# One change at the hand-over from attention to feed-forward, in a two-layer transformer kernel on one core

## The chip, the cores and the metric

The kernel runs on one core of a Trainium2 chip. The core has five engines with a queue each, and every queue is worked off in order: TensorE (PE in the profile; its weight loads are listed apart as PEld), VectorE (DVE), ScalarE (ACT), GpSimd (POOL) and SyncE (SP), which here only issues transfers (DMAs). Matrix products land in PSUM, a memory of eight banks of 128 rows by 512 fp32 numbers; all other tiles lie in SBUF. The metric is the device time of one call in microseconds (us), and lower is better.

## What is computed

```python
x = x + A(layernorm(x)); x = x + B(layernorm(x))
x = x + A(layernorm(x)); x = x + B(layernorm(x))
# A: q = x@wq in 16 heads of 28; one k = x@wk and one v = x@wv for all heads
#    softmax(q k^T / sqrt(28)) v, heads side by side, @ wo
# B: (silu(x@w_gate) * (x@w_up)) @ w_down
```

x has 2048 rows (tokens) of 448 numbers; the feed-forward B is 1792 wide. Everything is fp32. The two layers have the same weights.

## The kernel before

The tokens are worked in four chunks (0 to 3) of 512, each of four tiles of 128 rows. Most products are made from numbers split in a high and a low part (names that end in h and l): high times high, high times low, low times high. The norm's output is turned over, so that features lie on the partitions; features 384 to 447 are the fourth block of a chunk's tile `xh`. There the high parts fill rows 0 to 63 and the low parts rows 64 to 127, and in the feed-forward a second copy of the high parts in rows 64 to 127 of another tile, `xd`, serves the upper half of the array.

**Attention.** For each chunk and each of four groups of four heads the kernel runs eight cycles, 128 cycles per layer (`cycle`). A cycle takes two tiles of 128 keys (y = 0 and 1). `tile_scores` (L640) makes the scores of four heads at once in four row strips of PE: three heads go to a PSUM tile of three banks (a "three"), the fourth to a bank of its own (a "single"). DVE copies each single to SBUF (`pair`, L661); ACT takes the exponential of the three (L662) of y = 0, of the three of y = 1, and then of both singles together (L663), in place. `pv` (L695) follows one cycle later with the product of the exponentials and the values, into one bank: for each key tile the three first, and then its half of the pair. DVE adds the bank to the group's sum `o` (L703). When a group's last cycle is done, `post` normalises it: a small DMA spreads the row sums (`rs`, L717), DVE takes the reciprocal, a DMA writes it to DRAM (`rd`, L727), another brings it back broadcast over the rows (L728), POOL multiplies (L734), four DMAs move rows between groups (L748), and POOL splits the result (`onh`, `onl`, L135 and L136). The product with `wo` can then run.

**Hand-over.** When the last cycle's `pv` is issued, the last group of chunk 3 still has that whole chain ahead of it. Meanwhile PE does work of the feed-forward on chunk 0, whose norm was made long before: `unit(0, 0, 0)` and `unit(0, 0, 1)`, with full-height products (L312). Behind the second stand the down product of the first unit (`down`, in two steps: the first right there, the second held back in `left`), the `wo` product of chunk 3's groups 0 to 2, the second step, the `wo` product of group 3, and the addition to x (L611). Then `rest` begins: DVE takes the norm's statistics of chunk 3 (L217, L218), POOL the factor 1/sqrt(variance + eps) of its four tiles (L222 and the power, L223), DVE applies it (L230) and turns the tiles (L268), and a DMA sends them out to come back feature-wise. POOL makes chunk 2's parts out of a load issued earlier. `begin` makes chunk 1's parts. The copies `xd` of chunks 0 and 1 are made by two DMAs (L127) at the head of `rest`.

**Feed-forward.** 14 blocks (`fc`) of 128 hidden features, in 7 groups of two; for each group all four chunks, and for each chunk two units. A unit makes gate and up (L332: 64-row products, two at a time in the lower and upper half of the array), ACT the SiLU (L1024), DVE the product with up (L1025), ACT the high part (L1028), DVE the low part (L1031). `down` makes h times w_down into four banks, one for each token tile: two steps of twelve 64-row products, lower and upper half side by side on different banks; after the first step four tiny ACT copies (`between`, L339) read the banks, since the second step uses the same banks from the other half. `self.flip`, turned over at each call, says which banks begin in the lower half. After a group's second unit the four banks are added to x: tile 0 by DVE (L901), tile 2 by an ACT copy (L904) and POOL (L905), tile 1 by DVE, tile 3 again by ACT and POOL. `by_tile` (L888) is the same down product in full rows, twelve products of 128 rows, tile after tile; before the change it serves only the very last group of the program.

The order on each engine is the order in which the Python code issues; nothing re-orders it. A tile pool that takes over the space of a closed pool makes the first user of the new tile wait for the last users of the old one. The program also holds a second, exact version of the forward pass behind a branch that these inputs don't take.

Of the kernel before, what the change touches and what calls it, by code (L numbers as in the profile page):

```python
# [55 lines left out]
def forward(  # L56
# [69 lines left out]
    def dma(dst, src):  # L126
        nc.sync.dma_start(dst.bitcast(F32), src.bitcast(F32))  # L127
# [82 lines left out]

    def norm_steps(c, pool=pers, twice=True):

        got = {}
        cs = slice(4 * c, 4 * c + 4)

        def stat(t):
            nc.vector.bn_stats(stats[:, 4 * c + t, :], xres[:, 4 * c + t, :])  # L217
            nc.vector.bn_aggr(mv[:, 4 * c + t, :], stats[:, 4 * c + t, :])  # L218

        def scale():  # L220
            rstd = pers.tile([P, 4], F32, name="rstd", bufs=2)
            nc.gpsimd.tensor_scalar(rstd, mv[:, cs, 1], 1.0, EPS, ALU.mult, ALU.add)  # L222
            nc.gpsimd.tensor_tensor(rstd, rstd, halfn, ALU.pow)  # L223
            got["r"] = rstd

# [7 lines left out]

        fs = [lambda t=t: stat(t) for t in range(4)] + [scale]
        return fs + [lambda t=t: apply(t) for t in range(4)], got
# [107 lines left out]
    class Attention:  # L343
# [229 lines left out]
        def scores(self, ff, xb):  # L573
            next(switch)
            inner = ExitStack()
            with tc.tile_pool(name=f"ow{self.layer}", bufs=1, side="right", reuse_waits="tile") as ow:
# [73 lines left out]
                pairs = [wp.tile([P, 2, 512], F32, name=f"pair{y}") for y in range(2)]  # L650

                def singles(m):

                    return banks[6 + m % 2], banks[7 - m % 2]

                def cycle(m):

                    es, copies, pair = [], [], pairs[m % 2]
                    for y, one in enumerate(singles(m)):
                        pt, pt1 = tile_scores(2 * m + y, threes[y], one)  # L660
                        copies.append(nc.vector.tensor_copy(pt1, one))  # L661
                        es.append(nc.scalar.activation(pt, threes[y], AF.Exp, scale=SCALE))  # L662
                    es.append(nc.scalar.activation(pair, pair, AF.Exp, scale=SCALE))  # L663
                    exps[m] = [e.ins for e in es]
# [125 lines left out]
                aside[NT // 2 * 15 + 5] = lambda: ff.fetch(1)  # L790
                last = NT // 2 * len(GR)
                for m in range(last):
# [33 lines left out]
                ff.begin(xb)  # L826
                due.pop(min(due))()
                ff.unit(0, 0, 0)
                due.pop(min(due))()
# [16 lines left out]
    class FeedForward:  # L846
# [6 lines left out]
        def down(self, fs, fc, d, hh, hl):  # L853


            _, _, dh, dl = self.W[fc]
            if self.layer == 1 and d is self.dn.get(NC - 1) and fs is groups[-1]:
                return [lambda: self.by_tile(fs, fc, d, ((hh, dh), (hh, dl), (hl, dh))), lambda: None]
            self.flip = 1 - self.flip
# [197 lines left out]
        def begin(self, xb):  # L1057

            self.x1p = xb.enter_context(tc.tile_pool(name=f"x1{self.layer}", bufs=1, reuse_waits="tile"))
            self.X[1] = xtile(self.x1p)  # L1060
            halved(self.X[1], self.got.pop(1), range(4), nc.scalar.copy, nc.vector.tensor_tensor)

        def rest(self, xb):
            self.stage = xb.enter_context(tc.tile_pool(name=f"stage{self.layer}", bufs=2, reuse_waits="tile"))
            self.xbp = xb.enter_context(tc.tile_pool(name=f"xb{self.layer + 1}", bufs=2, reuse_waits="tile"))
            xd = xb.enter_context(tc.tile_pool(name=f"xd{self.layer}", bufs=1, reuse_waits="tile"))
            self.xd = [xd.tile([P, 512], F32R, name=f"xd{c}") for c in range(NC)]
            for c in range(2):
                dma(self.xd[c][64:128, :], self.X[c][0][0:64, 3, :])
                self.X[c] = (*self.X[c][:2], self.xd[c])  # L1070
            t3 = ExitStack()
            own = t3.enter_context(tc.tile_pool(name=f"t3{self.layer}", bufs=1, reuse_waits="tile"))
            tb = own.tile([P, D // 32, P], F32, name="tb3")
            fs3, got = norm_steps(3, own, twice=False)
            for f in fs3[:5]:
# [118 lines left out]
```

## Time and profile before

| | us |
|---|---|
| median of 3 runs (lowest to highest) | 1949.36 (1948.67 to 1949.93) |
| the profiled execution | 1949.26 |
| its span, first to last instruction | 1947.5 |
| hand-over of layer 0, from the last `pv` to the first steady unit | about 555 to 595 of the span |
| hand-over of layer 1 | about 1518 to 1558 |

Times in the profile count from the first instruction. A row of the timeline gives start, duration, engine, line, operation, output<-inputs with shape, and in brackets how long the engine had stood idle and whom it waited for. Matmul durations are modelled: they overlap, so PE's pace is read from the distance between starts.

### The profile page before, as it was taken

To read this page: it belongs to the slowest core of one execution; us is meant where nothing else is said; L and a number is where in the kernel's file an instruction comes from. 1 tells how busy PE (TensorE), PEld (TensorE's weight loads), DVE (VectorE), ACT (ScalarE), POOL (GpSimd) and SP (SyncE) were. 2 spreads that over 40 slices of the span, in tenths; PEclk is the share of its full clock that TensorE was granted. 3 is DMA by queue.
4 is the path that set the end of the run, shared out by engine and by line. 5 is a ranking of instruction groups with operands and counts; after the bars stand their busy time and mean duration, and the time that the engine had idled before them with its cause. 6 is when DMAs were issued, how large, how long until landed. Compare 5 with 4: busy or idle time off the path is not lost. (4 is left out here: it accounts for less than half of the span.)

```text
span 1947.5 us, 43868 instructions
## 1 busy us (share of the span) xinstructions
PE 1934.0 (99%) x18393; PEld 1311.6 (67%) x18393; DVE 980.8 (50%) x1675; ACT 1251.9 (64%) x1871; POOL 560.1 (29%) x596
## 2 busy tenths in 40 slices
PE   9999999999999999999999999999999999999998
PEld 7544545445468999999974445454454688888887
DVE  6665575665754222322666555757657432232223
ACT  4899898998953333333359998989989333333332
POOL 4213123122215333433341221122231352333420
PEclk9999999999999999999999999999999999999999
DMA  5111011021122011100251110110221220011102
GB/s 166 57 35 30 22 40 41 23 58 31 32 81 73 17 32 32 33 22 22 63 157 43 34 34 21 40 39 24 57 50 31 77 62 25 17 32 32 33 1 77
DMA packets 105475, 87.54 MB, mean 45 GB/s; under 512 B 25304, under 2 KB 85464, under 8 KB 105272
## 3 DMA queue, kind: packets, MB, share of 16 engines
q1 hardware_dynamic: 103576, 83.25, 15.5%
q8 instruction: 145, 2.38, 0.5%
q10 hardware_dynamic: 1696, 1.43, 0.2%
q14 instruction: 58, 0.48, 0.1%
HBM read 59.48 MB, written 23.33 MB: 43 GB/s over the span
## 5 line engine op out<-in xcount | busy, mean ns | idle before, releaser
L662 ACT ACTIVATE pt<-three 128x1536 f32<-128x1536 f32 x512 | 731.2, 1515 | 52.7 <-PE three L640 52.7
L695 PE MATMUL bank<-pt,vsb 128*32 128x512 f32 x3072 | 490.8, 598 | 0.0
L695 PE MATMUL bank<-pair,vsb 128*32 128x512 f32 x1024 | 487.4, 598 | 0.6 <-ACT pair L663 0.6
L640 PE MATMUL bank<-qstack,keys 32*128 32x512 f32 x1536 | 471.8, 425 | 0.0
L640 PE MATMUL three<-qstack,keys 32*128 32x512 f32 x4608 | 428.7, 408 | 0.5 <-ACT stage L546 0.3
L640 PEld LDWEIGHTS bank<-qstack,keys 32*128 32x128 f32 x1536 | 243.3, 183 | 248.1 <-issue 124.6
L661 DVE COPY pair<-bank 128x512 f32<-128x512 f32 x512 | 354.3, 692 | 95.1 <-PE bank L640 60.0
L332 PE MATMUL bank<-xh,wgh 64*128 64x512 f32 x1712 | 357.4, 389 | 0.0
L1025 DVE TENSOR_TENSOR sg<-bank,sg 128x512 f32<-128x512 f32 x112 | 77.4, 691 | 485.4 <-ACT sg L1024 474.7
L332 PE MATMUL bank<-xh,wgl 64*128 64x512 f32 x1391 | 310.7, 390 | 0.0
L332 PE MATMUL bank<-wdh,h 64*128 64x448 f32 x1760 | 303.3, 363 | 1.0 <-DVE h L1031 0.6
L663 ACT ACTIVATE pair<-pair 128x1024 f32<-128x1024 f32 x256 | 289.6, 1131 | 0.0
L640 PEld LDWEIGHTS three<-qstack,keys 32*128 32x128 f32 x4608 | 261.8, 183 | 14.2 <-DVE xres L611 1.5
L332 PE MATMUL bank<-xl,wgh 64*128 64x512 f32 x1284 | 268.5, 389 | 0.0
L695 PEld LDWEIGHTS bank<-pt,vsb 128*32 128x32 f32 x3072 | 101.7, 109 | 246.2 <-issue 153.2
L905 POOL TENSOR_TENSOR xres<-stage,xres 128x448 f32<-128x448 f32 x107 | 126.7, 1204 | 480.5 <-ACT stage L904 480.2
L703 DVE TENSOR_TENSOR o<-bank,o 128x512 f32<-128x512 f32 x224 | 155.0, 692 | 202.3 <-PE bank L695 202.3
L339 ACT COPY seen<-bank 128x1 f32<-128x1 f32 x654 | 74.9, 164 | 253.3 <-PE bank L332 252.7
L1024 ACT ACTIVATE sg<-bank 128x512 f32<-128x512 f32 x112 | 67.2, 600 | 215.9 <-PE bank L332 210.8
L332 PEld LDWEIGHTS bank<-xh,wgh 64*128 64x128 f32 x1712 | 182.0, 184 | 18.4 <-issue 1.0
L332 PEld LDWEIGHTS bank<-wdh,h 64*128 64x128 f32 x1760 | 183.2, 184 | 15.5 <-issue 1.7
L332 PE MATMUL bank<-wdl,h 64*128 64x448 f32 x880 | 174.7, 367 | 0.0
(149 smaller groups left out, 2105.8 us busy)
## 6 DMA issues: line engine op xcount, KB each, us to landing
o<-rd SPq DMA_DIRECT2D x32, 256.0 KB
qraw<-qd SPq DMA_DIRECT2D x128, 56.0 KB
xt<-tb SPq DMA_DIRECT2D x32, 224.0 KB
wdr<-in_B_w_down_dram SPq DMA_DIRECT2D x28, 224.0 KB
xn<-xt SPq DMA_DIRECT2D x8, 768.0 KB
wr<-in_B_w_gate_dram SPq DMA_DIRECT2D x28, 192.0 KB
wr<-in_B_w_up_dram SPq DMA_DIRECT2D x28, 192.0 KB
qd<-stage SPq DMA_DIRECT2D x20, 224.0 KB
```

Source lines behind the costliest of these rows:

```text
L332: nc.tensor.matmul(po, a, b, start=start, stop=stop, skip_group_check=True)
L339: nc.scalar.copy(seen[:, i : i + 1], po[:, 0:1])
L640: nc.tensor.matmul(three[:, j, :] if j < 3 else one, k[js, kp, ks], q[js, part, :], start=(z == 0), stop=(z == 2), tile_position=(32 * j, 0),)
L661: copies.append(nc.vector.tensor_copy(pt1, one))
L662: es.append(nc.scalar.activation(pt, threes[y], AF.Exp, scale=SCALE))
L663: es.append(nc.scalar.activation(pair, pair, AF.Exp, scale=SCALE))
L695: nc.tensor.matmul(to[32 * j : 32 * j + 32, :], vsb[:, n % NT, :], pts[n][j], start=(y == 0), stop=(y == 1), skip_group_check=True,)
L703: f = nc.vector.tensor_tensor(accs[i][:, 0, :], to, accs[i][:, 0, :], ALU.add)
L905: nc.gpsimd.tensor_tensor(r, s, r, ALU.add)
L1024: nc.scalar.activation(in_order(sg, True), natural(pg[0], True), AF.Silu)
L1025: nc.vector.tensor_tensor(in_order(sg, True), natural(pg[1], True), in_order(sg, True), ALU.mult)
```

## The change

Four edits at the hand-over, in both layers alike.

1. In the last cycle of a layer the exponential of the two singles is issued between those of the two threes, instead of behind both.
2. The factors of chunk 3's norm (`norm_steps(..., each=True)`) are made tile by tile, each right behind its tile's statistics: four times two POOL instructions on one column, instead of two on four columns.
3. The two DMAs that make `xd` of chunks 0 and 1 move up from the head of `rest`: chunk 0's into `begin`, chunk 1's behind the first step of the last group's `post` chain. The pool of the `xd` tiles is opened in `begin` with them, and so lies in other space.
4. The first down product of a layer (block 0, chunk 0) is made by `by_tile` in one step, and nothing of it is held back. `self.flip` isn't turned in that call, so from there on each down product of the layer starts with the other assignment of banks to halves.

```diff
-    def norm_steps(c, pool=pers, twice=True):
+    def norm_steps(c, pool=pers, twice=True, each=False):
...
-        def scale():
-            rstd = pers.tile([P, 4], F32, name="rstd", bufs=2)
-            nc.gpsimd.tensor_scalar(rstd, mv[:, cs, 1], 1.0, EPS, ALU.mult, ALU.add)
-            nc.gpsimd.tensor_tensor(rstd, rstd, halfn, ALU.pow)
-            got["r"] = rstd
+        def scale(t0=0, n=4):
+            if "r" not in got:
+                got["r"] = pers.tile([P, 4], F32, name="rstd", bufs=2)
+            r = got["r"][:, t0 : t0 + n]
+            nc.gpsimd.tensor_scalar(r, mv[:, 4 * c + t0 : 4 * c + t0 + n, 1], 1.0, EPS, ALU.mult, ALU.add)
+            nc.gpsimd.tensor_tensor(r, r, halfn[:, 0:n], ALU.pow)
...
-        fs = [lambda t=t: stat(t) for t in range(4)] + [scale]
+        if each:
+            fs = [lambda t=t: (stat(t), scale(t, 1)) for t in range(4)] + [lambda: None]
+        else:
+            fs = [lambda t=t: stat(t) for t in range(4)] + [scale]
...
                         copies.append(nc.vector.tensor_copy(pt1, one))
+                        if y and m == last - 1:
+                            nc.scalar.activation(pair, pair, AF.Exp, scale=SCALE)
                         es.append(nc.scalar.activation(pt, threes[y], AF.Exp, scale=SCALE))
-                    es.append(nc.scalar.activation(pair, pair, AF.Exp, scale=SCALE))
+                    if m < last - 1:
+                        es.append(nc.scalar.activation(pair, pair, AF.Exp, scale=SCALE))
...
                 ff.begin(xb)
                 due.pop(min(due))()
+                ff.above(1)
                 ff.unit(0, 0, 0)
...
             if self.layer == 1 and d is self.dn.get(NC - 1) and fs is groups[-1]:
                 return [lambda: self.by_tile(fs, fc, d, ((hh, dh), (hh, dl), (hl, dh))), lambda: None]
+            if fc == 0 and d is self.dn[0]:
+                return [lambda: self.by_tile(fs, fc, d, ((hh, dh), (hh, dl), (hl, dh))), lambda: None]
             self.flip = 1 - self.flip
...
         def begin(self, xb):
 
             self.x1p = xb.enter_context(tc.tile_pool(name=f"x1{self.layer}", bufs=1, reuse_waits="tile"))
+            xd = xb.enter_context(tc.tile_pool(name=f"xd{self.layer}", bufs=1, reuse_waits="tile"))
+            self.xd = [xd.tile([P, 512], F32R, name=f"xd{c}") for c in range(NC)]
+            self.above(0)
             self.X[1] = xtile(self.x1p)
             halved(self.X[1], self.got.pop(1), range(4), nc.scalar.copy, nc.vector.tensor_tensor)
+
+        def above(self, c):
+
+            dma(self.xd[c][64:128, :], self.X[c][0][0:64, 3, :])
 
         def rest(self, xb):
...
-            xd = xb.enter_context(tc.tile_pool(name=f"xd{self.layer}", bufs=1, reuse_waits="tile"))
-            self.xd = [xd.tile([P, 512], F32R, name=f"xd{c}") for c in range(NC)]
             for c in range(2):
-                dma(self.xd[c][64:128, :], self.X[c][0][0:64, 3, :])
                 self.X[c] = (*self.X[c][:2], self.xd[c])
...
-            fs3, got = norm_steps(3, own, twice=False)
+            fs3, got = norm_steps(3, own, twice=False, each=True)
```

What moves on the engines, at three places of layer 0 (layer 1 reads the same).

ACT at the end of the scores, before: `pt3` and `pair1` are the exponentials of the last second three and the last singles, the casts make chunk 1's parts, `sg` and `h2` are the two units' SiLU and high parts.

```order
L662 ACTIVATE pt3_811<-three1_798 128x1536
L663 ACTIVATE pair1_813<-pair1_813 128x1024
L292 CAST xh_6460<-xn_6344 128x512 x3
L296 CAST xh_6460<-xn_6344 128x512
L1024 ACT_TABLE_LOAD
L1024 ACTIVATE sg_6503<-bank1_6452 128x512
L1028 CAST h2_6502<-sg_6503 128x512
L1024 ACTIVATE sg_6541<-bank3_6454 128x512
L339 COPY seen_107<-bank4_6455 128x1
L339 COPY seen_107<-bank5_6456 128x1
L339 COPY seen_107<-bank6_78 128x1
L339 COPY seen_107<-bank7_79 128x1
```

The same place after the change:

```order
L668 ACTIVATE pair1_813<-pair1_813 128x1024
L669 ACTIVATE pt3_811<-three1_798 128x1536
L295 CAST xh_6468<-xn_6344 128x512 x3
L299 CAST xh_6468<-xn_6344 128x512
L1034 ACT_TABLE_LOAD
L1034 ACTIVATE sg_6512<-bank1_6452 128x512
L1038 CAST h2_6511<-sg_6512 128x512
L1034 ACTIVATE sg_6550<-bank3_6454 128x512
L1038 CAST h2_6549<-sg_6550 128x512
```

The singles' exponential stands one place earlier, and the four copies between the two steps of the first down product are gone.

SP at the hand-over, before: `rs`, `rd`, `o<-rd` and `o<-moved` are the last group's chain, `xn<-xt_2` the load of chunk 2.

```order
L717 DMA rs<-o_6170 128x1x16
L727 DMA rd<-rs 128x16
L728 DMA o_6170<-rd 128x1x512
L748 DMA o_6170<-moved_3_5628 4x512 x4
L130 DMA xn<-xt_2_818 128x3x512
L132 DMA xn<-xt_2_818 64x512 x2
L127 DMA xd_6636<-xh 64x512
L127 DMA xd_6637<-xh 64x512
L274 DMA xt_3_6666<-tb_6645 32x14x128 x4
```

And after:

```order
L725 DMA rs<-o_6170 128x1x16
L127 DMA xd_6463<-xh 64x512
L735 DMA rd<-rs 128x16
L736 DMA o_6170<-rd 128x1x512
L127 DMA xd_6464<-xh 64x512
L756 DMA o_6170<-moved_3_5628 4x512 x4
L130 DMA xn<-xt_2_818 128x3x512
L132 DMA xn<-xt_2_818 64x512 x2
L277 DMA xt_3_6656<-tb_6629 32x14x128 x4
```

The two copies now stand inside the chain, one ahead of `rd`, one ahead of `moved`.

POOL at the norm of chunk 3, with what each row waits for, before:

```order
L136 TENSOR_TENSOR onl<-o_6170,onh 128x512 [waits Pool_49]
L222 TENSOR_SCALAR rstd<-mv 128x4 [waits DVE_49]
L223 TENSOR_TENSOR rstd<-rstd,halfn 128x4 [waits Pool_49]
L1083 COPY applied<-xn 128x1 [waits DVE_49,PE_49]
L292 CAST xh<-xn 128x512 [waits DMAHW7_49,Activation_49]
```

And the last of the factors and what follows, after:

```order
L223 TENSOR_SCALAR rstd<-mv 128x1 [waits DVE_49]
L224 TENSOR_TENSOR rstd<-rstd,halfn 128x1 [waits Pool_49]
L1097 COPY applied<-xn 128x1 [waits DVE_49,PE_49]
L295 CAST xh<-xn 128x512 [waits DMAHW1_49,Activation_49]
L296 TENSOR_TENSOR xl<-xn,xh 128x512 [waits Pool_49]
```

Four such pairs stand there now, each waiting for its own tile's statistics; on DVE each application waits for its own factor, in the order of before.

3 lines of the change are left out of this document (1 added, 2 removed).

## The prediction

> **What bounds the kernel now.** I read the page first, then the groups of instructions for what PE waited for, then the timeline of both hand-overs, engine by engine.
>
> ```profile
> PE 1934.0 (99%) x18393; PEld 1311.6 (67%) x18393; DVE 980.8 (50%) x1675; ACT 1251.9 (64%) x1871; POOL 560.1 (29%) x596
> ...
> L695 PE MATMUL bank<-pair,vsb 128*32 128x512 f32 x1024 | 487.4, 598 | 0.6 <-ACT pair L663 0.6
> ...
> L332 PE MATMUL bank<-wdh,h 64*128 64x448 f32 x1760 | 303.3, 363 | 1.0 <-DVE h L1031 0.6
> ```
>
> PE is busy for 99% of the span, and among its large groups only two show idle time that another engine ended: a singles' exponential, and a low part of h. Both stand at the two hand-overs. So the change can act on a few us of 1949, and each of its terms is read from starts on PE there. I work out layer 0 and check layer 1.
>
> **Edit 1, the singles' exponential.** ACT and DVE at the end of the scores:
>
> ```profile
> 551.69 1.08 ACT L663 ACTIVATE pair<-pair 128x1024 f32<-128x1024 f32 x1
> 552.64 2.81 ACT L662 ACTIVATE pt<-three 128x1536 f32<-128x1536 f32 x2
> 555.31 1.09 ACT L663 ACTIVATE pair<-pair 128x1024 f32<-128x1024 f32 x1
> ```
> ```profile
> 553.48 0.69 DVE L661 COPY pair<-bank 128x512 f32<-128x512 f32 x1 [0.21 <-PE bank L640]
> ```
> ```profile
> 553.98 1.47 ACT L662 ACTIVATE pt<-three 128x1536 f32<-128x1536 f32 x1
> ```
>
> And PE, up to the first product of the feed-forward (L312):
>
> ```profile
> 556.45 0.62 PE L695 MATMUL bank<-pair,vsb 128*32 128x512 f32 x1 [0.30 <-ACT pair L663]
> ...
> 557.33 1.02 PE L695 MATMUL bank<-pair,vsb 128*32 128x512 f32 x2
> 558.28 0.50 PE L312 MATMUL bank<-xh,wgh 128*128 128x512 f32 x1
> ```
>
> PE stands until the singles' exponential ends (555.31 + 1.09 = 556.40). After that the strip of the singles still has four passes, 0.44 apart (556.45 and 557.33 are two apart), and the product starts 1.83 after the release. In the new order the singles' exponential waits for the second copy (553.48 + 0.69 = 554.17), so it starts at 554.22 in place of the three's 553.98; the three follows 0.95 later (551.69 to 552.64), at 555.17, and ends 1.47 later at 556.64. PE is released at 556.69, 0.24 later than now, but the singles of the first key tile are then done, so two passes remain instead of four: 1.83 - 0.88 = 0.95, and the product starts at 557.64. Gain: 0.64, taken as 0.6. DVE's last addition to `o`, and with it the last group's chain, starts earlier by the same amount.
>
> **Edit 4, the first down in full rows.** PE around the two steps (the first starts at 568.48, the second between the rows of 575.88 and 577.60):
>
> ```profile
> 568.16 0.39 PE L312 MATMUL bank<-xh,wgl 128*128 128x512 f32 x1
> 568.48 0.47 PE L332 MATMUL bank<-wdh,h 64*128 64x448 f32 x2
> ...
> 569.82 0.36 PE L628 MATMUL bank<-woh,onh 64*128 64x448 f32 x2
> ...
> 575.88 0.37 PE L619 MATMUL bank<-woh,onl 128*128 128x448 f32 x1
> ...
> 577.60 0.47 PE L619 MATMUL bank<-woh,onh 128*128 128x448 f32 x1
> 577.91 0.36 PE L619 MATMUL bank<-wol,onh 128*128 128x448 f32 x1
> ```
>
> And the first and last of the 24 full-row products at the program's end:
>
> ```profile
> 1936.92 0.37 PE L888 MATMUL bank<-wdh,h 128*128 128x448 f32 x1
> ...
> 1941.64 0.37 PE L888 MATMUL bank<-wdh,h 128*128 128x448 f32 x1
> ```
>
> Before: 1.66 from the last gate product to `wo`, 1.72 less one pace of 0.20 around the second step, and 0.11 more between the next two starts (0.31 for 0.20): 3.29. After: one pace of 0.23, twelve full rows at (1941.64 - 1936.92) / 23 = 0.205, that is 2.46, and one change from full to half rows, 0.2 (0.09 more than a pace from 568.16 to 568.48, and a longer second start as above): 2.89. Gain: 0.4, from two changes of the array's shape that go away. The full rows wait for the same h as the first step. The four ACT copies that go away cost nothing, since ACT is idle there. The second unit's high part must now wait for the full rows, until about 570.3; it is needed past 582. The turned `flip` swaps which bank begins in which half, in all later steps; each step still fills tiles 0 and 2 first and then 1 and 3, so I price it at nothing, with 0.2 either way over both layers.
>
> **Edit 3, the upper copies.** SP, PE, and a start of the same kind where nothing waits:
>
> ```profile
> 580.33 1.13 SPq L127 DMA_DIRECT2D xd<-xh  x2
> ```
> ```profile
> 580.23 0.50 PE L332 MATMUL bank<-xh,wgh 64*128 64x512 f32 x2
> ...
> 583.23 0.49 PE L332 MATMUL bank<-xd,wgl 64*128 64x512 f32 x1 [0.16 <-DMA xd<-xh]
> ```
> ```profile
> 1559.32 0.40 PE L332 MATMUL bank<-xh,wgh 64*128 64x512 f32 x2
> ```
> ```profile
> 1565.60 0.60 ACT L1024 ACTIVATE sg<-bank 128x512 f32<-128x512 f32 x1 [1.96 <-PE bank L332]
> ```
> ```profile
> 587.29 0.61 ACT L1024 ACTIVATE sg<-bank 128x512 f32<-128x512 f32 x1 [1.96 <-PE bank L332]
> ...
> 595.66 0.60 ACT L1024 ACTIVATE sg<-bank 128x512 f32<-128x512 f32 x1 [1.97 <-PE bank L332]
> ...
> 602.95 0.60 ACT L1024 ACTIVATE sg<-bank 128x512 f32<-128x512 f32 x1 [1.96 <-PE bank L332]
> ```
>
> From a unit's first product to its SiLU it is 1565.60 - 1559.32 = 6.28 where nothing waits, and 587.29 - 580.23 = 7.06 in chunk 1's first unit. Less 0.11 for the change of shape, 0.67 is the wait for `xd`, which was issued at 580.33. Moved up, the copies are issued about 559 and 565, and are there long before. Gain: 0.67.
>
> What the copies are moved past: on SP the first stands ahead of `rd`, the second ahead of `moved`. Each takes some 0.57 to issue (1.13 for two) and falls in a stretch in which SP waits for DVE or POOL anyway. The first also waits for the last users of the space that it takes, the exponentials and `pv`, which are over by then. Their transfers run beside those of the chain:
>
> ```profile
> 564.04 0.55 SPq L728 DMA_DIRECT2D o<-rd  x1
> ```
> ```profile
> 575.29 1.29 POOL L136 TENSOR_TENSOR onl<-o,onh 128x512 fp32r<-128x512 f32 x1
> ```
>
> The chain ends at 575.29 + 1.29 = 576.58, and PE takes it up at 577.60: 1.0 of slack. After edits 1 and 4 the chain is 0.6 earlier and PE 1.0, so 0.6 of slack remains. The second copy can cost the broadcast between nothing and the 2.9 that both took from issue to use (580.33 to 583.23). I take nothing, since it is issued behind the broadcast of 564.04; 2.9 would cost PE 2.3 per layer.
>
> **Edit 2, the factors.** The chain that PE meets in chunk 1's second unit:
>
> ```profile
> 582.99 0.18 DVE L218 BATCH_NORM_AGGREGATE mv<-stats 128x2 f32<-128x6 f32 x1
> ...
> 583.72 0.18 DVE L218 BATCH_NORM_AGGREGATE mv<-stats 128x2 f32<-128x6 f32 x1
> 585.33 1.78 DVE L230 TENSOR_SCALAR xn<-xres,mv,rstd 128x448 f32<-128x448 f32 x4 [1.43 <-POOL rstd L223]
> ...
> 589.17 0.65 DVE L1025 TENSOR_TENSOR sg<-bank,sg 128x512 f32<-128x512 f32 x1
> ```
> ```profile
> 583.99 0.20 POOL L222 TENSOR_SCALAR rstd<-mv 128x4 f32<-128x4 f32 x1 [7.41 <-DVE mv L218]
> 584.27 1.02 POOL L223 TENSOR_TENSOR rstd<-rstd,halfn 128x4 f32<-128x4 f32 x1
> 587.24 0.19 POOL L1083 COPY applied<-xn 128x1 f32<-128x1 f32 x1 [1.95 <-DVE xn L230]
> ```
>
> DVE has the statistics at 583.90, waits 1.43 for the factors, applies and turns until 589.2, and only then takes the SiLU's product (L1025), whose input ACT gave at 587.90. So h and the additions that free the banks come late, and PE waits: the SiLUs of 587.29 and 595.66 are 8.37 apart, against 7.29 from 595.66 to 602.95. That is a stall of 1.08.
>
> The price of the power on one column isn't in the trace. It lies between the copy of one column (0.19) and the four-column power (1.02). The multiply-add on four columns takes 0.20, so I read 0.20 as what any small POOL instruction costs and (1.02 - 0.20) / 4 = 0.205 as the price of a column: 0.40 for one. A pair then takes 0.28 (583.99 to 584.27) + 0.40 = 0.68, less than the 0.73 between statistics. With all PE work ahead 1.0 earlier, the statistics end at 582.90, the last factor is there at 582.99 + 0.68 = 583.67, and the applications run through from 582.80 to 584.58 instead of to 587.11: the chain is 2.53 earlier. PE's need of it is 0.6 + 0.4 + 0.67 = 1.67 earlier. So the stall shrinks by 0.86, to 0.22. POOL's work on chunk 2 behind the factors moves up with them.
>
> One thing speaks against this edit. An application and a POOL instruction can get in each other's way:
>
> ```profile
> 256.38 1.29 POOL L136 TENSOR_TENSOR qstack<-qraw,qstack 128x512 fp32r<-128x512 f32 x1
> ```
> ```profile
> 256.62 1.29 DVE L230 TENSOR_SCALAR xn<-xres,mv,rstd 128x448 f32<-128x448 f32 x1
> ```
>
> The application that takes 0.45 (1.78 for four) took 1.29 beside a POOL instruction, and ended just after it. If two applications hold up the last tile's pair in the same way, that is 0.9, of which 0.4 is covered, since the last application would not start before 584.1 anyway. The chain is then 2.0 earlier instead of 2.53, and the layer gains 2.0. The SBUF page of the Trainium skill ("SBUF — State Buffer", Who interferes with whom) states this as a rule: VectorE in its two-port modes and GpSimd share a pair of ports, and whoever starts first keeps it for the whole instruction. By that rule the hold-up would come, with the 1945.3 of the first rival below; the row at 256.62 agrees with it.
>
> **Sum.** 0.6 + 0.4 + 0.67 + 0.86 = 2.53 per layer. Layer 1 has the same stalls:
>
> ```profile
> 1549.98 0.60 ACT L1024 ACTIVATE sg<-bank 128x512 f32<-128x512 f32 x1 [1.96 <-PE bank L332]
> ...
> 1558.31 0.60 ACT L1024 ACTIVATE sg<-bank 128x512 f32<-128x512 f32 x1 [1.96 <-PE bank L332]
> ```
>
> 8.33 between the SiLUs, so a stall of 1.04 for 1.08. Two layers give 5.1. The profiled execution took 1949.26 (span 1947.5 and 1.76 around it), 0.1 under the median of 1949.36: 1949.26 - 5.1 = 1944.2.
>
> **The rivals.**
> - *Hold-ups on POOL and DVE.* Applications and factors hold each other up as above, or a power of one column costs 0.55 to 0.9. From 0.55 on each 0.1 puts the last factor 0.4 later than 584.1, and all of it reaches PE. With the hold-up alone 2.0 per layer, 1945.3; with a power of 0.7 the last factor is there at 580.80 + 4 x 0.98 = 584.7, 1.9 per layer, 1945.5; with 0.9 at 585.5, 1.1 per layer, 1947.0. For it: the row at 256.62. Against: these POOL instructions are short.
> - *The power has a fixed price of 1.02.* A pair takes 1.30, four take 5.2 from 580.80 (the statistics stand 0.73 apart and end at 582.90, so the first are there at 580.71, and POOL starts 0.09 later), the last factor is there at 586.0 and its application ends at 586.5 instead of 587.11. As all that follows hangs on it, 0.6 per layer remains of everything, 1948.0. For it: only four columns were ever measured.
> - *Slower: fixed price and hold-ups together on the one chain.* Three applications between the pairs, 0.45 each, put its end at 587.8, 0.7 later than now: 1950.7. It decides from a pair price of 1.46, hold-ups included, since (586.66 - 580.80) / 4 = 1.46.
> - *The copies hurt the chain, or the order does not give what it says.* If the broadcast lands 2.9 later, 0.2 per layer remains: 1948.9.
>
> **How the numbers follow.** The forecast case, a power near 0.4, gets 0.56: 1944.2, with 1943.6 if the rest of the stall goes too. Hold-ups get 0.22 (1945.3 to 1947.0), the fixed price 0.10 (1948.0), the slower rival 0.05, copies and surprises 0.07. The range from 1943.6 to 1948.1 holds the first three. A measurement of this kernel can hardly tell less than 0.2% (3.9 us) from no change; that bound stands at 1945.5. Below it lies nearly all of the forecast case and little else, 0.55; within 0.2% the others, 0.42; slower by more than that only by a surprise, 0.03.
>
> **What would show it.** On PE, the singles' row without a wait, the second three's row with one, and the first L312 start 2.5 after the last three on ACT begins. Twelve full-row products of 0.205 ahead of `wo`, and no second step. `xd` issued near 559 and 565, and no PE row that waits for it. On POOL four short pairs; the power's duration on one column is the number on which most hangs. The SiLUs of chunk 1 then stand 7.5 apart. Wrong would be: powers near 1 us, a `wo` row of group 3 that waits for POOL, or a changed pace of the steady units, 7.29.

## The result and the profile after

The changed kernel takes 1946.11 us (median of 20 runs, 1945.15 to 1948.73) against 1949.26 for the kernel before (20 runs, 1948.32 to 1950.11). The ratio is 0.9985 with a 95% interval of 0.9979 to 0.9991. It is 3.2 us faster where 5.1 was forecast. That is 0.15%, less than the 0.2% taken as the bound, but the interval lies wholly below 1.

The profiled execution took 1948.05, nearly 2 above the median of its kernel. Those 2 us lie in its first 20 us and have nothing to do with the change; the last section comes back to them. So starts in the two traces are compared from a common row, the last but one exponential of a pair in layer 0's scores: 551.69 before and 553.68 after, 1.99 apart. "Less 1.99" below means a start of the changed kernel set back to the old scale.

The groups of instructions of the changed kernel, and ACT around the first hand-over (start, duration, engine and line, operation, tiles, and in brackets the wait ahead and what ended it):

```profile
PE 1933.1 (99%) x18369; PEld 1325.7 (68%) x18369; DVE 978.1 (50%) x1675; ACT 1256.8 (65%) x1863; POOL 563.8 (29%) x608
...
L703 PE MATMUL bank<-pt,vsb 128*32 128x512 f32 x3072 | 490.8, 598 | 0.6 <-ACT pt L669 0.6
...
L335 PE MATMUL bank<-wdh,h 64*128 64x448 f32 x1728 | 320.8, 363 | 0.8 <-DVE h L1041 0.4
```
```profile
553.68 1.06 ACT L671 ACTIVATE pair<-pair 128x1024 f32<-128x1024 f32 x1
554.65 1.45 ACT L669 ACTIVATE pt<-three 128x1536 f32<-128x1536 f32 x1
556.26 1.06 ACT L668 ACTIVATE pair<-pair 128x1024 f32<-128x1024 f32 x1 [0.17 <-DVE pair L666]
557.23 1.43 ACT L669 ACTIVATE pt<-three 128x1536 f32<-128x1536 f32 x1
...
567.54 0.60 ACT L1034 ACTIVATE sg<-bank 128x512 f32<-128x512 f32 x1 [1.04 <-PE bank L315]
...
587.73 0.60 ACT L1034 ACTIVATE sg<-bank 128x512 f32<-128x512 f32 x1 [1.97 <-PE bank L335]
...
595.89 0.60 ACT L1034 ACTIVATE sg<-bank 128x512 f32<-128x512 f32 x1 [1.96 <-PE bank L335]
```

The wait for a singles' exponential has become one for a three's, and the wait for the low part of h is still in the groups. From the common row to the SiLU of chunk 1's second unit it was 595.66 - 551.69 = 43.97 and is 595.89 - 553.68 = 42.21: layer 0's hand-over is 1.76 shorter, where 2.53 was forecast. Layer 1's, measured between the same two rows, went from 43.99 to 42.18, 1.81 shorter. PE shows where it was gained:

```profile
557.38 0.62 PE L703 MATMUL bank<-pair,vsb 128*32 128x512 f32 x1
...
558.71 0.63 PE L703 MATMUL bank<-pt,vsb 128*32 128x512 f32 x3 [0.29 <-ACT pt L669]
...
559.71 0.50 PE L315 MATMUL bank<-xh,wgh 128*128 128x512 f32 x1
...
569.61 0.40 PE L315 MATMUL bank<-xh,wgl 128*128 128x512 f32 x1
569.84 0.37 PE L898 MATMUL bank<-wdh,h 128*128 128x448 f32 x1
...
572.10 0.37 PE L898 MATMUL bank<-wdh,h 128*128 128x448 f32 x1
572.40 0.47 PE L631 MATMUL bank<-woh,onh 64*128 64x448 f32 x2
...
581.33 0.50 PE L335 MATMUL bank<-xh,wgh 64*128 64x512 f32 x2
...
592.13 1.00 PE L335 MATMUL bank<-wdh,h 64*128 64x448 f32 x4 [0.22 <-DVE h L1041]
```

| stretch, layer 0 | before | after | gain | forecast |
|---|---|---|---|---|
| common row to the first feed-forward product | 6.59 | 6.03 | 0.56 | 0.6 |
| last product of the second unit to chunk 1's first | 12.07 | 11.72 | 0.35 | 0.4 |
| chunk 1's first product to its SiLU | 7.06 | 6.40 | 0.66 | 0.67 |
| that SiLU to the next | 8.37 | 8.16 | 0.21 | 0.86 |

Three stretches did almost what was forecast. The fourth did not: the stall of chunk 1's second unit is 0.87 (8.16 for 7.29), not 0.22. The engines ahead of it, DVE and POOL of the changed kernel:

```profile
584.81 0.18 DVE L217 BATCH_NORM_AGGREGATE mv<-stats 128x2 f32<-128x6 f32 x1
584.91 1.49 DVE L230 TENSOR_SCALAR xn<-xres,mv,rstd 128x448 f32<-128x448 f32 x3
586.84 0.51 DVE L230 TENSOR_SCALAR xn<-xres,mv,rstd 128x448 f32<-128x448 f32 x1 [0.43 <-POOL rstd L224]
587.26 2.22 DVE L271 STREAM_TRANSPOSE tb<-xn 128x448 f32<-128x448 f32 x4
589.40 0.65 DVE L1035 TENSOR_TENSOR sg<-bank,sg 128x512 f32<-128x512 f32 x1
```
```profile
582.89 0.19 POOL L223 TENSOR_SCALAR rstd<-mv 128x1 f32<-128x1 f32 x1 [4.84 <-DVE mv L217]
583.17 0.55 POOL L224 TENSOR_TENSOR rstd<-rstd,halfn 128x1 f32<-128x1 f32 x1
583.80 0.19 POOL L223 TENSOR_SCALAR rstd<-mv 128x1 f32<-128x1 f32 x1
584.08 0.56 POOL L224 TENSOR_TENSOR rstd<-rstd,halfn 128x1 f32<-128x1 f32 x1
...
584.99 0.86 POOL L224 TENSOR_TENSOR rstd<-rstd,halfn 128x1 f32<-128x1 f32 x1
...
586.21 0.59 POOL L224 TENSOR_TENSOR rstd<-rstd,halfn 128x1 f32<-128x1 f32 x1
```

A power of one column takes 0.55, not 0.40. Pairs start 0.91 apart (582.89 to 583.80), statistics 0.73 apart, so POOL falls behind, and the last factor is there at 586.80, 1.81 after the last statistics (584.99) instead of 0.77. The application to the last tile waits for it, the transposes follow, and the SiLU's product (L1035) starts 1.07 after its SiLU is done (588.33). That product now starts at 589.40 less 1.99 = 587.41, 1.76 earlier than before (589.17). This is exactly the gain of the hand-over.

The two hand-overs gave 1.76 + 1.81 = 3.57. Against that stands a loss of 0.31 near the end of layer 0, where a unit's SiLU comes 7.95 after the one before it instead of 7.64. It shows a wait of PE that the kernel before doesn't have there:

```profile
965.92 0.50 PE L335 MATMUL bank<-xh,wgh 64*128 64x512 f32 x2 [0.38 <-ACT seen L342]
```

ACT reaches that copy late, since it first splits a chunk (L295, L299) whose loads it waited for until 965.12. 3.57 - 0.31 = 3.26, beside the 3.15 between the medians. That these agree so closely is partly luck: from layer 0's last SiLU to the common row of layer 1 the changed kernel's trace is 0.43 longer, and from layer 1's last SiLU to the end 0.44 shorter, and over the 14 traces of this document these two stretches vary by 1.6 and 0.6.

### The profile page after: what moved, and what is told of

It is laid out like the page before. It is cut to its first block, busy times and chain, and to the rows that moved or that the text cites. A ratio compares the mean times of both kernels' runs of the same rounds, so it can differ in the third digit from the quotient of the medians.

```text
span 1946.3 us, 43775 instructions
## 1 busy us (share of the span) xinstructions
PE 1933.1 (99%) x18369; PEld 1325.7 (68%) x18369; DVE 978.1 (50%) x1675; ACT 1256.8 (65%) x1863; POOL 563.8 (29%) x608
## 5 line engine op out<-in xcount | busy, mean ns | idle before, releaser
L669 ACT ACTIVATE pt<-three 128x1536 f32<-128x1536 f32 x512 | 722.1, 1478 | 52.9 <-PE three L643 52.8
L335 PE MATMUL bank<-xh,wgh 64*128 64x512 f32 x1712 | 439.0, 389 | 0.4 <-ACT seen L342 0.4
L335 PE MATMUL bank<-xh,wgl 64*128 64x512 f32 x1391 | 363.8, 390 | 0.0
L335 PE MATMUL bank<-xl,wgh 64*128 64x512 f32 x1284 | 329.5, 389 | 0.0
L1035 DVE TENSOR_TENSOR sg<-bank,sg 128x512 f32<-128x512 f32 x112 | 77.3, 690 | 486.8 <-ACT sg L1034 476.3
L335 PE MATMUL bank<-wdh,h 64*128 64x448 f32 x1728 | 320.8, 363 | 0.8 <-DVE h L1041 0.4
L671 ACT ACTIVATE pair<-pair 128x1024 f32<-128x1024 f32 x254 | 277.6, 1093 | 0.0
L335 PEld LDWEIGHTS bank<-xh,wgh 64*128 64x128 f32 x1712 | 260.9, 184 | 15.2 <-issue 1.0
L335 PEld LDWEIGHTS bank<-wdh,h 64*128 64x128 f32 x1728 | 238.4, 184 | 12.4 <-DVE h L1041 1.2
L335 PEld LDWEIGHTS bank<-xh,wgl 64*128 64x128 f32 x1391 | 214.9, 184 | 12.6
L335 PE MATMUL bank<-wdl,h 64*128 64x448 f32 x864 | 212.0, 366 | 0.0
```

The lines of the kernel that those rows point to most:

```text
L335: nc.tensor.matmul(po, a, b, start=start, stop=stop, skip_group_check=True)
L1035: nc.vector.tensor_tensor(in_order(sg, True), natural(pg[1], True), in_order(sg, True), ALU.mult)
```

## The experiments

**Theory A, one chain.** Chunk 1's second unit gets its h and its banks from DVE's chain: residual, statistics, factors, applications, transposes, SiLU's product. The end of that chain sets the end of the hand-over. What only brings PE there earlier (edit 3) is then worth nothing; edit 2 is worth all by which it shortens the chain; edits 1 and 4 count because they bring PE and the chain forward alike. **Theory B, terms that add:** each edit is worth what the table above shows in its stretch.

Each of the three sets of four kernels ran on one chip with the kernel before, which had a median of 1949.15, 1947.80 and 1948.69 in them. Times are therefore given as a difference from the kernel before of the same set. The ratios' intervals are some 1.8 us to either side, as wide as most effects looked for, so the verdict rests on SiLU rows of the trace. Their steady distance is 7.29 in every kernel, and the two layers of one kernel agree within 0.13. Distances can be 0.01 off by rounding. The differences are between medians; the ratios are estimates of their own, so the two can stand 0.0002 apart.

| kernel | 2nd SiLU to 3rd | 3rd to 4th | sum, layer 0 | sum, layer 1 | us against before | ratio (95%) |
|---|---|---|---|---|---|---|
| before | 21.20 | 8.37 | 29.57 | 29.55 | | |
| after | 20.19 | 8.16 | 28.35 | 28.33 | -3.2 | 0.9985 (0.9979 to 0.9991) |
| x1, after without edit 2 | 20.27 | 9.03 | 29.30 | 29.17 | -2.0 | 0.9992 (0.9983 to 1.0001) |
| x2, after without edit 3 | 20.98 | 7.48 | 28.46 | 28.33 | -4.0 | 0.9982 (0.9973 to 0.9991) |
| x3, after, transposes later | 20.27 | 7.29 | 27.56 | 27.56 | -4.9 | 0.9978 (0.9969 to 0.9987) |
| x4, after, factors 2 + 1 + 1 | 20.27 | 8.03 | 28.30 | 28.30 | -3.8 | 0.9980 (0.9971 to 0.9989) |
| y1, edit 2 alone | 21.21 | 7.53 | 28.74 | 28.70 | -2.0 | 0.9990 (0.9981 to 0.9999) |
| y2, edit 3 alone | 20.55 | 8.99 | 29.54 | 29.54 | +0.2 | 0.9998 (0.9989 to 1.0007) |
| y3, before, transposes later | 21.21 | 7.29 | 28.50 | 28.52 | -1.7 | 0.9990 (0.9981 to 0.9999) |
| y4, x3 without edit 2 | 20.27 | 7.29 | 27.56 | 27.55 | -5.1 | 0.9972 (0.9962 to 0.9982) |
| z1, edit 1 alone | 21.19 | 8.34 | 29.53 | 29.54 | -1.6 | 0.9989 (0.9980 to 0.9998) |
| z2, edit 4 alone | 20.97 | 8.31 | 29.28 | 29.29 | -0.7 | 0.9994 (0.9985 to 1.0003) |
| z3, edit 4, halves not turned | 20.83 | 8.35 | 29.18 | 29.22 | -0.5 | 0.9996 (0.9987 to 1.0006) |
| z4, y4 without edit 3 | 20.99 | 7.29 | 28.28 | 28.21 | -3.8 | 0.9978 (0.9969 to 0.9987) |

The 2nd SiLU belongs to chunk 0's second unit, the 3rd and the 4th to chunk 1's two units. Edit 1 acts ahead of these rows; the other edits and the experiments act between them.

### x1: the factors at once again

```diff
-            fs3, got = norm_steps(3, own, twice=False, each=True)
+            fs3, got = norm_steps(3, own, twice=False)
```

> Changed kernel with edit 2 undone: the factors of chunk 3 again in one pair for all four tiles. Theory A, one chain: in chunk 1 PE's second unit waits for DVE's chain (residual, statistics, factors, applications, transposes, then the SiLU's product), whose applications ended 1.69 earlier in the changed kernel, 0.84 of it because all PE work ahead came earlier and 0.85 because of the factors. Without them the SiLUs of chunk 1 stand 8.16 + 0.85 = 9.0 apart and the time is 2 x 0.85 = 1.7 above the changed kernel, 1947.8. Theory B, terms that add: edit 2 is worth only what the distance of those two SiLUs lost (8.37 to 8.16), so 8.4 apart and 0.4 above, 1946.5.

ACT and DVE of this kernel:

```profile
585.63 0.60 ACT L1034 ACTIVATE sg<-bank 128x512 f32<-128x512 f32 x1 [1.97 <-PE bank L335]
...
594.67 0.60 ACT L1034 ACTIVATE sg<-bank 128x512 f32<-128x512 f32 x1 [1.97 <-PE bank L335]
```
```profile
584.36 1.78 DVE L230 TENSOR_SCALAR xn<-xres,mv,rstd 128x448 f32<-128x448 f32 x4 [1.42 <-POOL rstd L224]
586.06 2.22 DVE L271 STREAM_TRANSPOSE tb<-xn 128x448 f32<-128x448 f32 x4
588.20 0.65 DVE L1035 TENSOR_TENSOR sg<-bank,sg 128x512 f32<-128x512 f32 x1
```

9.03 and 9.01 apart, as A expected, not 8.4. Inside the changed kernel edit 2 carries 0.95 in layer 0 and 0.84 in layer 1, though its own stretch had shown 0.21. (0.12 of layer 0's 0.95 is the slower of two paces of the `wo` product, see z2 below; without it edit 2 is worth 0.83 here too.) The product starts 588.20 - 585.63 = 2.57 behind its SiLU's start, against 1.67 in the changed kernel. The time, 1.2 above the changed kernel's -3.2, lies on A's side within wide intervals.

### x2: the copies back in their old place

```diff
         def begin(self, xb):
...
-            self.above(0)
...
         def rest(self, xb):
...
             for c in range(2):
+                self.above(c)
                 self.X[c] = (*self.X[c][:2], self.xd[c])
```

(The tiles of `xd` are made in `rest` again, and the call of `above(1)` is gone.)

> Changed kernel with edit 3 undone: the two upper copies are issued in their old place again. Theory A: the wait for xd (0.67) comes back, but DVE's chain does not move, so the stall behind it shrinks by the same amount: start to SiLU 6.95, the two SiLUs 8.16 - 0.67 = 7.5 apart, time as of the changed kernel, 1946.1. Theory B: the wait comes back and the SiLUs stay 8.16 apart, 2 x 0.67 = 1.3 above, 1947.4.

PE and ACT of this kernel:

```profile
582.63 0.49 PE L335 MATMUL bank<-xd,wgl 64*128 64x512 f32 x1 [0.25 <-DMA xd<-xh]
```
```profile
565.72 0.60 ACT L1033 ACTIVATE sg<-bank 128x512 f32<-128x512 f32 x1 [1.04 <-PE bank L315]
586.70 0.60 ACT L1033 ACTIVATE sg<-bank 128x512 f32<-128x512 f32 x1 [2.15 <-PE bank L335]
594.18 0.60 ACT L1033 ACTIVATE sg<-bank 128x512 f32<-128x512 f32 x1 [1.97 <-PE bank L335]
```

The wait for `xd` is back and delays the third SiLU by 0.8, and the next stall is shorter by nearly as much: 28.46 and 28.33 in all, against 28.35 and 28.33. In the changed kernel the early copies gain nothing: the 0.11 of layer 0 stands in the `wo` product ahead of the wait (see z2 below), and layer 1 has 0.00. The time is no longer than the changed kernel's either (-4.0 and -3.2, intervals that overlap).

### x3: the transposes behind chunk 1's first unit

```diff
-            for t in range(4):
-                turn_tile(got, tb, t)
...
-            send(tb, self.raw[3])
+
+            def turn():
+                for t in range(4):
+                    turn_tile(got, tb, t)
+                send(tb, self.raw[3])
+                self.fetch(3)
+
...
-            self.soon.append([0, lambda: self.fetch(3)])
+            self.soon.append([0, turn])
```

> Changed kernel, but chunk 3's four transposes on DVE, their sending and the fetch stand behind chunk 1's first unit instead of ahead of it, so 2.22 of DVE's chain leaves the path to that unit's SiLU product. Theory A: the product starts right after the SiLU; the SiLUs of chunk 1 stand 7.3 to 7.5 apart instead of 8.16, 2 x 0.7 to 0.87 below the changed kernel, 1944.4 to 1944.7. Rival: what holds the second unit is the low part of h, which took 1.29 beside POOL's split instead of 0.69; it stays beside POOL, so about 0.5 of the stall stays, 7.8 apart, 1945.4. A second rival: the later sending makes chunk 3's fetch or the weights behind it late, and PE waits in chunk 2 or 3: 1946 or more.

DVE of this kernel:

```profile
586.65 0.69 DVE L1035 TENSOR_TENSOR sg<-bank,sg 128x512 f32<-128x512 f32 x1 [0.97 <-ACT sg L1034]
...
588.07 0.96 DVE L1041 TENSOR_TENSOR h<-sg,h 128x512 fp32r<-128x512 f32 x1 [0.20 <-ACT h L1038]
...
589.49 2.21 DVE L271 STREAM_TRANSPOSE tb<-xn 128x448 f32<-128x448 f32 x4
```

DVE now waits for the SiLU (0.97) and not PE for DVE. The SiLUs stand 7.29 apart in both layers: the whole stall is gone, the sum is 0.79 and 0.77 shorter, and nothing in chunks 2 and 3 gave it back. The low part of h still took 0.96, beyond its usual 0.69, and in y4 below it took 1.24 with the stall gone all the same, so being slowed there was not the cause of the stall. The time is 4.9 below the kernel before.

### x4: factors for two tiles, then one, then one

```diff
-            fs = [lambda t=t: (stat(t), scale(t, 1)) for t in range(4)] + [lambda: None]
+            fs = [lambda t=t: (stat(t), t and scale(max(t - 1, 0) if t == 1 else t, 2 if t == 1 else 1)) for t in range(4)] + [lambda: None]
```

> Changed kernel with the factors in three pairs: tiles 0 and 1 together, then 2, then 3. By the powers seen on POOL (1.02 on four columns, 0.55 on one: 0.39 + 0.16 a column) the last factor comes 1.1 behind the last statistics instead of 1.81, since POOL is no longer behind when they arrive. Theory A with POOL's price as the cause: the applications end 0.4 to 0.5 earlier, the SiLUs stand 7.7 apart, 1945.2. Rival: the hold-up between applications and powers (0.86 for 0.55) sets the end, whichever way the columns are grouped: 8.0 to 8.2 apart, 1946.

DVE and POOL of this kernel:

```profile
582.92 1.33 DVE L230 TENSOR_SCALAR xn<-xres,mv,rstd 128x448 f32<-128x448 f32 x3
```
```profile
581.64 0.19 POOL L223 TENSOR_SCALAR rstd<-mv 128x2 f32<-128x2 f32 x1 [5.84 <-DVE mv L217]
581.91 0.70 POOL L224 TENSOR_TENSOR rstd<-rstd,halfn 128x2 f32<-128x2 f32 x1
582.70 0.19 POOL L223 TENSOR_SCALAR rstd<-mv 128x1 f32<-128x1 f32 x1
582.97 0.55 POOL L224 TENSOR_TENSOR rstd<-rstd,halfn 128x1 f32<-128x1 f32 x1
583.61 0.27 POOL L223 TENSOR_SCALAR rstd<-mv 128x1 f32<-128x1 f32 x1
583.96 0.70 POOL L224 TENSOR_TENSOR rstd<-rstd,halfn 128x1 f32<-128x1 f32 x1
```

The expected 0.4 to 0.5 did not come: 8.03 apart, 0.05 and 0.03 less in sum than the changed kernel, and inside the 8.0 to 8.2 of the rival. The expectation had overlooked that the pair for tiles 0 and 1 ends only at 582.61, so the one for tile 2 starts at 582.70, and POOL is behind again when tile 3 arrives. The rival has a share as well: beside the applications the last pair took 0.27 and 0.70, where 0.19 and 0.55 are usual, 0.23 more. But the power for tile 2, which began 0.05 behind an application, took its usual 0.55, so the run does not settle when a POOL instruction is held up. It does give a price: two columns take 0.70, as 0.39 + 0.16 a column says.

### y1 and y2: edit 2 alone, edit 3 alone

On the kernel before, y1 takes over the changed `norm_steps` and its call, and y2 only this, with the pool of the `xd` tiles opened in `begin` as well:

```diff
         def begin(self, xb):
...
+            self.above(0)
...
                 ff.begin(xb)
                 due.pop(min(due))()
+                ff.above(1)
                 ff.unit(0, 0, 0)
```

> Kernel before with edit 2 alone. Theory A, one chain: the factors bring DVE's chain 0.85 earlier, PE's need of it does not move, so the SiLUs of chunk 1 stand 8.37 - 0.85 = 7.5 apart and the two layers gain 1.7 against the kernel before, 1947.5. Theory B, terms that add: the edit is worth what the distance lost in the whole change, 8.37 to 8.16, so 0.4, 1948.8.

> Kernel before with edit 3 alone. Theory A: the first unit's products need not wait for xd, its SiLU comes 0.67 earlier, and the second unit waits that much longer for the chain, which has not moved: SiLUs 8.37 + 0.67 = 9.0 apart, time as of the kernel before, 1949.2. Theory B: 8.4 apart and 2 x 0.67 = 1.3 below, 1947.8.

ACT of edit 3 alone (y2):

```profile
565.48 0.60 ACT L1025 ACTIVATE sg<-bank 128x512 f32<-128x512 f32 x1 [1.03 <-PE bank L312]
586.03 0.60 ACT L1025 ACTIVATE sg<-bank 128x512 f32<-128x512 f32 x1 [1.96 <-PE bank L332]
595.02 0.60 ACT L1025 ACTIVATE sg<-bank 128x512 f32<-128x512 f32 x1 [1.97 <-PE bank L332]
```

Both went as A expected: 7.53 and 7.48 for edit 2 (7.5 expected), 8.99 and 8.98 for edit 3 (9.0 expected). Edit 3 brings the third SiLU 0.65 forward, the stall behind it grows by 0.62, and the time does not move (+0.2). Edit 2 by itself gains 0.83 to 0.85 per layer, where the prediction's 0.86 had been meant to come on top of edit 3's 0.67.

### y3 and y4: the transposes later, without edit 2

y3 is the kernel before with the diff of x3, y4 is x3 with the diff of x1.

> Kernel before, but chunk 3's four transposes, their sending and the fetch stand behind chunk 1's first unit. Theory A: the applications end at 587.1, before the SiLU at 587.9, so nothing of the stall of 1.08 is left: SiLUs 7.3 apart, 2 x 1.06 below the kernel before, 1947.0. Rival: without the factors by tile the chain is still too late for h's low part and the additions to the residual, 7.7 apart, 1947.9.

> Changed kernel with the later transposes of x3_turn_later and with edit 2 undone. Theory A: the applications end 0.85 later than in x3_turn_later, where the SiLU's product stood 0.97 behind them, so edit 2 is worth nothing there: SiLUs 7.3 apart, time as of x3_turn_later, 1944.3. Theory B: edit 2 is worth a fixed sum wherever it stands, 0.4 (distance) to 1.7 (without it in the changed kernel), so 1944.7 to 1946.0.

DVE of y4:

```profile
583.91 1.78 DVE L230 TENSOR_SCALAR xn<-xres,mv,rstd 128x448 f32<-128x448 f32 x4 [1.42 <-POOL rstd L224]
585.83 0.69 DVE L1035 TENSOR_TENSOR sg<-bank,sg 128x512 f32<-128x512 f32 x1
```

No stall is left in either (7.29). In y4 the applications and the SiLU (585.20 + 0.60 = 585.80) end together and the product starts at once: edit 2, worth 0.84 or more per layer in the changed kernel, is worth 0.00 here (27.56 and 27.56 with it, 27.56 and 27.55 without). On the kernel before, moving the transposes alone gains 1.07 and 1.03 per layer, more than edit 2. y4 is 5.1 below the kernel before, at a ratio of 0.9972. Its hand-overs are 0.79 and 0.78 shorter than the changed kernel's; the intervals of the two ratios still touch.

### z1 to z4: edits 1 and 4 alone, and edit 3 with the chain out of the way

z1 is the kernel before with edit 1, z2 is the kernel before with edit 4 as the change writes it. In z3 the full-row step takes its turn in the order of the halves too, so that the later steps keep theirs:

```diff
             self.flip = 1 - self.flip
+            if fc == 0 and d is self.dn[0]:
+                return [lambda: self.by_tile(fs, fc, d, ((hh, dh), (hh, dl), (hl, dh))), lambda: None]
             one, two = ((0, 1), (2, 3)) if self.flip else ((2, 3), (0, 1))
```

z4 is y4 with the diff of x2.

> Kernel before with edit 1 alone. Theory A, one chain: the scores end earlier for PE and for DVE's chain alike, so nothing is taken back later: all of it counts. By PE's rows in the changed kernel 0.55 per layer from the last exponentials to the second SiLU of the feed-forward (15.73 to 15.18), SiLUs of chunk 1 8.37 apart as before, 1.1 below the kernel before. The prediction's 0.64 would give 1.3. Rival: the three's later exponential delays the last group's chain and shows as a wait at the output projection: 0 to 0.5.

> Kernel before with edit 4 alone (the halves of all later steps turned, as in the changed kernel). Theory A: 0.35 per layer between the second SiLU and that of chunk 1's first unit (21.20 to 20.85), for PE and DVE's chain alike, SiLUs of chunk 1 8.37 apart, 0.7 below the kernel before. Rival: the turned halves cost the 0.31 that the changed kernel lost at layer 0's last but one unit (960 us), so 0.4 below.

> As z2_full_rows_alone, but the full-row step takes its turn in the order of the halves, so that all later steps keep the order that they had before. Theory A: the same as z2_full_rows_alone, 0.7 below. Rival (the turned halves cost 0.31 at 960 us): 0.7 here and 0.4 there.

> y4_turn_later_at_once (changed kernel, transposes later, factors at once) with edit 3 undone. Theory A: with the transposes out of the way DVE's chain no longer sets the second unit, so PE's wait for xd counts in full, where it counted nothing in x2_copies_back and y2_copies_alone: the first SiLU of chunk 1 0.7 later, SiLUs 7.3 apart, 1.3 to 1.4 above y4_turn_later_at_once. Theory C, the copies are worth nothing anywhere: the same as y4_turn_later_at_once.

z1: 1.6 below the kernel before, no new wait behind it (8.34 between the SiLUs); in layer 0 the way from the scores to the second SiLU is 0.58 shorter. z2 gains 0.29 and 0.26 in the two layers, z3 0.39 and 0.33. The difference is not shown to be a cost of the turned halves. It stands in the `wo` product behind the full rows: from its first 128-row product to its last it takes 7.33 in both layers of z2 and 7.20 in both of z3, but x1, which turns the halves in both layers, has 7.33 in layer 0 and 7.20 in layer 1, and the changed kernel, which turns them too, has 7.20 in both. Chunk 1's first product starts 0.12 later in z2 for that reason, and without it z2 is no longer than z3 in either layer. All kernels with edit 4 show one of these two paces; what sets it was not found. The 0.31 at 960 us is not theirs: there z2 is 0.28 longer than the kernel before and z3 0.20, with either order. ACT of z4:

```profile
565.43 0.60 ACT L1033 ACTIVATE sg<-bank 128x512 f32<-128x512 f32 x1 [1.03 <-PE bank L315]
586.42 0.60 ACT L1033 ACTIVATE sg<-bank 128x512 f32<-128x512 f32 x1 [2.15 <-PE bank L335]
593.72 0.60 ACT L1033 ACTIVATE sg<-bank 128x512 f32<-128x512 f32 x1 [1.97 <-PE bank L335]
```

The third SiLU is 0.72 later than in y4 and nothing behind it gives that back: 28.28 and 28.21 for 27.56 and 27.55. The time is 1.3 above y4 by the two differences, as A expected and against theory C, though the intervals of the two ratios overlap. The same edit was worth 0.03 and 0.01 per layer on the kernel before and, without the pace of `wo`, nothing in the changed kernel.

Theory A gave the distance of chunk 1's SiLUs within 0.1 in all kernels but x4, for which the arrival of the factors had been worked out wrongly. Theory B is out: the table by stretches shows where a gain appears, not which edit made it.

## Why the prediction was right and wrong

**Direction and range.** The kernel got faster, and 1946.1 lies in the range; the forecast time, 1944.2, is missed by 1.9 of the 5.1 forecast, and the result falls on the other side of the 0.2%.

**Edit 1: right.** Less 1.99, the singles' exponential starts at 554.27 (554.22 forecast), the second three's at 555.24 (555.17), PE is released at 556.72 (556.69), and the product starts at 557.72 (557.64). 0.56 of 0.6 came, and 0.58 to 0.60 alone (z1).

**Edit 4: right.** From the first of the twelve full rows to the last it is 2.26 (569.84 to 572.10), 0.205 a step. 0.35 of 0.4 came, and 0.33 to 0.39 alone (z3). No run shows a cost of the turned halves, which the prediction had put at nothing.

**Edit 3: mechanism right, worth wrong.** No row of PE waits for `xd`, and start to SiLU is 6.40 for a forecast of 6.39. The copies did not hurt the group's chain either. But the 0.67 was no gain of this edit: x2 and y2 show that DVE's chain takes it back at the next unit, and only z4 against y4 shows it in full. The prediction's sum wasn't wrong for that reason, since it had set the stall that remains so that all terms together came to the chain's 2.53. It was wrong to give 0.67 of these to a step that doesn't shorten the chain.

**Edit 2: the step that failed.** "I read 0.20 as what any small POOL instruction costs and (1.02 - 0.20) / 4 = 0.205 as the price of a column: 0.40 for one." The rows give 0.55 for one column, 0.70 for two, 1.02 for four, so 0.39 fixed and 0.16 a column. That used up the slack of this step, but by itself no more: with a pair of 0.28 + 0.55 = 0.83 the prediction's sum has the last factor at 580.80 + 4 x 0.83 = 584.1, and before that the last application could not start anyway. The loss came from two terms that the sum had at nothing. POOL stands 0.08 between one pair and the next (583.72 to 583.80), so a pair takes 0.91 and not 0.68, which is more than the 0.73 between statistics, and each tile's factor comes later behind its statistics than the one before: three such gaps are 0.25. And beside the applications the third power took 0.86 and the fourth 0.59, 0.31 and 0.04 more than the 0.55. Together these are 0.60. The factors shorten the chain by 0.86 instead of 1.53 (1.76 and 2.53 less what the work ahead gave, 0.90 and 1.0). That is 0.67 less per layer, nearly all of it these 0.60, and 1.3 in all; the smaller terms fell short by 0.1 per layer, 0.2 in all, and 0.3 was lost at 960 us. Together 1.8 of the missing 1.9.

**The rivals.** The first one came, in both its halves: a power of 0.55 and a hold-up. Its prices for the one or the other, 1945.3 to 1947.0, hold the result. The Trainium skill's rule on the shared ports ("SBUF — State Buffer", Who interferes with whom) says that whoever issues first keeps them for its whole instruction. The traces agree only in part. In all four kernels with a factor for each tile (changed kernel, x2, x3 and y1) the third power began 0.08 to 0.10 behind an application, took 0.84 to 0.86, and ended 0.04 after the next application. But in x4 a power began 0.05 behind an application (582.97 after 582.92) and took its usual 0.55, although an application takes some 0.5; by the rule it would have been held up. So what sets the 0.31 is open. The fixed price of 1.02 and the slower rival built on it are out, and so is the later broadcast: from its issue to POOL's product it took 5.48, and 5.47 before.

**What stays open.** When a power is held up beside an application, and what sets the pace of the `wo` product (7.20 or 7.33). Then the 0.31 at 960 us: it came in the changed kernel, x1, x2, x4, z2 and z3 (0.20 to 0.33), less in z1 and y4 (0.16 and 0.11) and not in x3, y1, y2, y3 and z4. No single edit goes with it. In the changed kernel ACT waited there for loads; why they landed later was not tried.

## What to carry to other kernels

When PE's waits at a hand-over hang on one chain of another engine, price an edit by what it takes off that chain: an edit that only brings PE to the wait sooner is worth nothing until the chain is short, and then all of it. Look first for work on the chain that nobody there needs, such as the transposes of chunk 3, before making the needed work finer. A price for fewer columns must not be split off from one measured size; splitting a small instruction repeats its fixed part and the gap behind it.

## What the runs showed of the hardware

**A power on POOL has a fixed price beside that of its columns.** It takes 0.55 us for 128x1, 0.70 for 128x2 and 1.02 for 128x4, so some 0.39 and 0.16 a column, while the multiply-add ahead of it takes 0.19 to 0.20 for one, two or four columns (0.27 once in each layer of x4, beside an application).

**The first 20 us come in kinds that move the whole execution by 2 us.** This is where the profiled execution of the changed kernel lost its 2 us. Windows of 0 to 20 us, before and then after: length, busy time and number of instructions of PE, its weight loads, DVE, ACT and POOL, then the granted TensorE clock, the DMA share and GB/s.

```profile
0.00:20.00 20.00, 15.85 (x79) 13.32 (x80) 11.39 (x26) 7.52 (x14) 9.35 (x29) 0.91 0.78 250
```
```profile
0.00:20.00 20.00, 15.64 (x71) 12.88 (x72) 11.38 (x26) 6.57 (x12) 9.22 (x29) 0.83 0.75 237
```

PE had done 71 products for 79, at a mean clock of 0.83 for 0.91. Of the 14 profiled executions four had 0.83 (changed kernel, y1, y3, z3), and in these the last but two exponential of a three in layer 0's scores starts at 551.5 to 552.4; in the ten with 0.91 or 1.00 it starts at 549.4 to 550.6. No edit touches that stretch. Whether the clock or the loads come first was not separated. Who compares two profiles of this kernel by their spans compares this too, so stages have to be compared from a common row.
